# One decode step of attention and MLP: the last 256 KB of wo by six transfers in place of one

## The chip, the cores and the metric

The kernel runs on one core of a Trainium2 chip. The metric is the device time of one execution in microseconds (us); the kernel before takes 102.07 us, the median of 3 runs that lie between 102.06 and 102.33 us. A core has five engines that run their own instruction streams: TensorE (PE, the matmuls; PEld in the profile is its weight load), VectorE (DVE), ScalarE (ACT), GpSimd (POOL) and SyncE (SP, which here only issues transfers). Data comes from HBM into SBUF, which has 128 partitions, by 16 DMA engines that the profile counts together. Matmuls write to PSUM. Engines and transfers wait for one another by semaphores.

## The reference, cut to what matters

```
xn  = layernorm(x)                                # x: [1, 1, 1024]
q   = xn @ wq                                     # 32 heads of 128
k,v = the last 4096 positions of the caches       # 4 kv heads, 8 q heads each
p   = softmax(q k^T / sqrt(128))
o   = p v
A   = o @ wo                                      # wo: [4096, 1024]
y   = layernorm(xn)
h   = gelu(y @ w1 + b1)                           # w1: [1024, 3584]
B   = h @ w2 + b2                                 # w2: [3584, 1024]
out = x + A + B
```

All inputs are bf16. One token is decoded, so every weight and every cache row is used once.

## The kernel before, in words

All large inputs are loaded by SP, one transfer after the other on one queue, in this order: wq in 4 transfers, w1 in 4, the four K blocks, the four V blocks, then w2 in 4 and wo in 7. The first sixteen go out at once. w2 overwrites the buffer of w1 and wo the buffer WA that held wq, so SP waits at L285 until TensorE has finished with w1, and then issues the last eleven (L286, L287) through the helper `load_rows` (L133 to L140; its `dma_start` is L138 in the profile). The issue of the output (L458) comes behind them on the same queue.

`load_rows` gives each partition a run of rows that is contiguous in HBM. wo is seen as [128, 32, 1024]: partition p holds rows 32p to 32p+31, and transfer j brings `WO_CHUNKS[j]` of these 32 to all partitions. `WO_CHUNKS` is [8, 8, 8, 4, 2, 1, 1], so the last transfer brings one row of 1024 bf16 (2,048 bytes) to each of 128 partitions, 256 KB in all. Every transfer has its own semaphore, which stands at 16 when all of it has landed.

TensorE computes q and h as row products (L254), transposes K, takes the scores and, after the softmax, p times v. The output row is held as four pieces of 256 numbers in four groups of 32 PSUM partitions. `out_rows_mms` (L403 to L411, its matmul is L408) adds the products of one chunk of w2 or wo to it: it waits for the semaphore of the chunk and then does 4 matmuls for each row. The chunks of w2 come first (L420, L440, L449), those of wo last, in order (L451, L452). After the last matmul ScalarE copies the row out of PSUM (L456) and SP stores it (L458) and waits until it has landed (L459). The tail of the kernel is therefore: a chunk of wo lands, its matmuls run, and this seven times.

Of the kernel before, what the change touches and what calls it, by code (L numbers as in the profile page):

```python
# [9 lines left out]
D = 1024  # L10
# [12 lines left out]
W1_CHUNKS = [2, 2, 2, 2]  # L23
W2_CHUNKS = [9, 9, 8, 2]
WO_CHUNKS = [8, 8, 8, 4, 2, 1, 1]
PAD = 32


# [12 lines left out]
def bass_parallel_sum__sliding_block_cached__mixer_channel_mlp__decode_kernel(  # L41
# [18 lines left out]
    pe, dve, act, pool, sp = nc.tensor, nc.vector, nc.scalar, nc.gpsimd, nc.sync  # L60

    def sems(name, n):
        return [nc.alloc_semaphore(f"{name}{i}") for i in range(n)]
# [4 lines left out]
    s_k = sems("s_k", HKV)  # L68
    s_v = sems("s_v", HKV)
    s_wo = sems("s_wo", len(WO_CHUNKS))  # L70
    s_w2 = sems("s_w2", len(W2_CHUNKS))

    PE = Track(nc, "S_PE")
# [4 lines left out]
    def sb(name, shape, d):  # L78
        return nc.alloc_sbuf_tensor(name, shape, d)
# [23 lines left out]
    U2 = sb("U2", [128, FC], f32)  # L103
    GT = sb("GT", [128, FC + PAD], bf16)
    MXP = sb("MXP", [128, 32], f32)
    MX32 = sb("MX32", [32, 1], f32)
    DIAG = sb("DIAG", [32, 32], f32)
    NMB = sb("NMB", [128, 32], f32)
    Pb = sb("Pb", [128, HKV * NBLK * REP + PAD], bf16)
    SUMP = sb("SUMP", [128, 128], f32)  # L110
    REC = sb("REC", [128, 1], f32)
    ON = sb("ON", [128, DH], bf16)
    OT = sb("OT", [128, 32 + PAD], bf16)
    KV = sb("KV", [128, HKV * W + HKV * NBLK * DH], bf16)
# [3 lines left out]
    W2 = W1[:, 0:FC * D]  # L118
    WA = sb("WA", [128, KC * NQ], bf16)
# [10 lines left out]
    wo_p = A_wo.rearrange("(p j) n -> p j n", j=32)  # L130
# [4 lines left out]
    def load_rows(dst, src, chunks, width, semaphores):  # L135
        c0 = 0
        for j, n in enumerate(chunks):
            sp.dma_start(  # L138
                dst[:, c0 * width:(c0 + n) * width].rearrange("p (c n) -> p c n", c=n),
                src[:, c0:c0 + n, :],  # L140
            ).then_inc(semaphores[j], 16)
            c0 += n
# [31 lines left out]
    pool.wait_ge(POOL.sem, POOL.cnt)  # L174
    POOL.mark(pool.memset(GT[:, FC:FC + PAD], 0.0))
    pool.wait_ge(POOL.sem, POOL.cnt)
    POOL.mark(pool.memset(OT[:, 32:32 + PAD], 0.0))
    pool.wait_ge(POOL.sem, POOL.cnt)
# [92 lines left out]
    for h in range(HQ):  # L271
        last = pe.matmul(PSb[:, 7 * 1024 + 2 * h: 7 * 1024 + 2 * h + 1], lhsT=Qrow[0:1, h * 128:(h + 1) * 128],  # L272
                         rhs=identb[0:1, 0:1], is_transpose=True)
# [10 lines left out]

    sp.wait_ge(PE.sem, C["h"])  # L285
    load_rows(W2, w2_p, W2_CHUNKS, D, s_w2)  # L286
    load_rows(WA, wo_p, WO_CHUNKS, D, s_wo)  # L287


    KPAIRS = [[0, 1], [2, 3], [4, 5]]  # L290
# [36 lines left out]
    for u in range(NUNIT):  # L327
# [13 lines left out]
        for bb in range(16):  # L341
            o = banks[bb // 8] * 1024 + (bb % 8) * 128
            last = pe.matmul(PSb[:, o:o + 128], lhsT=KT[:, col + bb * 128: col + (bb + 1) * 128],  # L343
                             rhs=identb[:, :], is_transpose=True)
# [16 lines left out]
    for g in range(HKV):  # L361
        if g == HKV - 1:
            wait_kt(pe, 7)
        for b in range(NBLK):
            last = pe.matmul(  # L365
                PS[:, g * 256 + b * 8: g * 256 + (b + 1) * 8],
                lhsT=KT[:, g * W + b * 128: g * W + (b + 1) * 128], rhs=QT[:, g * 8:(g + 1) * 8])
# [32 lines left out]
    def acc(a):  # L400
        return PS[32 * a:32 * a + 32, 6 * 512:6 * 512 + 256]

    def out_rows_mms(weights, vec, chunks, semaphores, j, stop_at=None):  # L403
        c0 = sum(chunks[:j])
        pe.wait_ge(semaphores[j], 16)
        for c in range(c0, c0 + chunks[j]):
            for a in range(4):
                ins = pe.matmul(acc(a), lhsT=vec[:, c:c + 32],  # L408
                                rhs=weights[:, c * D + a * 256: c * D + (a + 1) * 256],
                                start=False, stop=(c == stop_at))  # L410
        return ins  # L411
# [4 lines left out]
    for a in range(4):  # L416
        pe.matmul(acc(a), lhsT=identb[0:1, 0:32], rhs=XBR[0:1, a * 256:(a + 1) * 256], start=True, stop=False)
        pe.matmul(acc(a), lhsT=identb[0:1, 0:32], rhs=XBR[0:1, D + a * 256:D + (a + 1) * 256], start=False, stop=False)
    pe.wait_ge(DVE.sem, C["d_GT"])
    out_rows_mms(W2, GT, W2_CHUNKS, s_w2, 0)  # L420
    pe.wait_ge(DVE.sem, C["sump"])
    C["tot"] = PE.mark(pe.matmul(PS[:, 3 * 512:3 * 512 + 1], lhsT=SUMP[:, :], rhs=onesf[:, 0:1]))
    dve.wait_ge(PE.sem, C["tot"])
# [4 lines left out]
    for g in range(HKV):  # L428
        pe.wait_ge(s_v[g], 16)
        for b in range(NBLK):  # L430
            i = g * NBLK + b
            last = pe.matmul(PS[32 * g:32 * g + 32, 4 * 512:4 * 512 + DH],  # L432
                             lhsT=Pb[:, i * REP:i * REP + 32], rhs=V[:, i * DH:(i + 1) * DH],
                             start=(b == 0), stop=(b == NBLK - 1))
# [2 lines left out]
    dve.wait_ge(DVE.sem, C["rec"])  # L437
    C["on"] = DVE.mark(dve.tensor_scalar(out=ON[:, :], in0=PS[:, 4 * 512:4 * 512 + DH], scalar1=REC[:, 0:1],
                                         scalar2=None, op0=ALU.mult))
    out_rows_mms(W2, GT, W2_CHUNKS, s_w2, 1)  # L440
    pe.wait_ge(DVE.sem, C["on"])
    for dq in range(4):
        last = pe.matmul(PS[:, 5 * 512:5 * 512 + 32], lhsT=E4[:, dq * 128:(dq + 1) * 128],
                         rhs=ON[:, dq * 32:(dq + 1) * 32], start=(dq == 0), stop=(dq == 3))
# [1 line left out]
    dve.wait_ge(PE.sem, C["o2"])  # L446
    C["OT"] = DVE.mark(dve.tensor_copy(OT[:, 0:32], PS[:, 5 * 512:5 * 512 + 32]))
    for j in range(2, len(W2_CHUNKS)):
        out_rows_mms(W2, GT, W2_CHUNKS, s_w2, j)  # L449
    pe.wait_ge(DVE.sem, C["OT"])  # L450
    for j in range(len(WO_CHUNKS)):  # L451
        last = out_rows_mms(WA, OT, WO_CHUNKS, s_wo, j, stop_at=31)  # L452
    C["fin"] = PE.mark(last)

    act.wait_ge(PE.sem, C["fin"])
# [34 lines left out]
```

## Time and profile before

| what | from | value |
|---|---|---|
| median of the runs | times | 102.07 us |
| span of the profiled execution (first to last instruction) | page | 100.8 us |
| time outside the span, median minus span | worked out | 1.27 us |
| bytes read from HBM | page | 39.86 MB, 395 GB/s over the span |
| TensorE busy | page | 69.3 us (69%) |
| idle time of TensorE before L408 with wo, waiting for transfers | groups of instructions | 9.9 us, 6 waits |
| last transfer of wo: SP starts its issue, it lands | timeline of SP, chain | 67.91 us, 98.24 us |
| first and last issue of the output store, end of the span | timeline of SP | 99.15 us, 100.8 us |

The profiled execution's own time is its span with what lies around it; the page gives the span alone, and the 1.27 us are taken as fixed. The page's second part cuts the span into 40 slices; its row DMA is the mean busy share of the 16 DMA engines, in tenths. In the groups of instructions the idle time before a group is put down to what ended it. Beside these views the trace has a record of every packet that a DMA engine moved (start, duration, bytes, queue, but not which of the 16 engines moved it) and of every increment of a transfer's semaphore.

### The profile page before, as it was taken

Reading aid. Unit: us, or ns where it says so; the run is one execution under the profiler, and the core shown is the slowest. Engines: PE = TensorE matmul, PEld = TensorE weight load, DVE = VectorE, ACT = ScalarE, POOL = GpSimd, SP = SyncE. Lnnn points to the kernel's source line nnn. Section 1 sums busy time; section 2 is a strip of 40 time slices with the busy share of each in tenths; the row PEclk is TensorE's granted clock in tenths of the full one; section 3 lists DMA queues with packets and bytes.
Section 4 is the critical chain, followed back from the end, with each engine's and each line's share of the span. In section 5 each row is a group of like instructions: output and inputs, shape, how many; then the busy total and the mean of one; then the engine's idle time right before and its main releaser. Section 6 shows DMA issues by size and latency. Waiting matters only on the chain.

```text
span 100.8 us, 1803 instructions
## 1 busy us (share of the span) xinstructions
PE 69.3 (69%) x825; PEld 42.7 (42%) x825; DVE 21.4 (21%) x46; ACT 13.8 (14%) x16; POOL 4.8 (5%) x18
## 2 busy tenths in 40 slices
PE   0002399999946999996799984649999934070781
PEld 0001233333304223331799984236999823040420
DVE  0003520000054000002876934555000200000000
ACT  0400060000051000002554740040000000000001
POOL 6740000000000000000000000000000000000000
PEclk9999999999996559999999997555559999555555
DMA  4899999999999999999999999999999999999930
GB/s 104 358 442 432 417 436 416 416 431 427 449 432 392 450 427 404 416 416 426 419 423 423 416 431 456 431 395 443 425 398 447 429 423 435 416 422 403 388 139 1
DMA packets 4194, 39.96 MB, mean 396 GB/s; under 512 B 726, under 2 KB 730, under 8 KB 1244
## 3 DMA queue, kind: packets, MB, share of 16 engines
q1 hardware_dynamic: 3896, 39.85, 94.2%
q8 instruction: 6, 0.10, 0.4%
q10 hardware_dynamic: 292, 0.01, 0.2%
HBM read 39.86 MB, written 0.00 MB: 395 GB/s over the span
## 4 chain that ended last, share of the span: by engine, by line
DMA 38%; PE 34%; SPq 20%; DVE 5%; issue 1%; ACT 1%
PE PS L254 31%; DMA WA<-in_A_wo_dram 30%; SPq L138 20%; DMA XB<-in_A_x_dram 7%; DVE ROW L264 2%; PE PS L272 1%; PE PS L234 1%; PE PS L217 1%; PE PS L408 0%; ACT ORow L456 0%; DVE XNT L225 0%; ACT msx L221 0%; DVE msx L198 0%; DVE msy L198 0%; DVE YT L230 0%
## 5 line engine op out<-in xcount | busy, mean ns | idle before, releaser
L254 PE MATMUL PS<-WA,XNTb 128*1 128x512 bf16 x64 | 16.4, 424 | 0.3 <-DVE msy L198 0.3
L254 PE MATMUL PS<-W,YTb 128*1 128x512 bf16 x56 | 15.0, 438 | 0.0
L408 PE MATMUL PS<-WA,OT 128*32 128x256 bf16 x128 | 7.3, 379 | 9.9 <-DMA WA<-in_A_wo_dram 9.9
L254 PEld LDWEIGHTS PS<-WA,XNTb 128*1 128x1 bf16 x64 | 5.8, 91 | 10.5 <-issue 3.5
L408 PEld LDWEIGHTS PS<-WA,OT 128*32 128x32 bf16 x128 | 3.8, 123 | 13.4 <-DMA WA<-in_A_wo_dram 10.3
L432 PE MATMUL PS<-KV,Pb 128*32 128x128 bf16 x128 | 9.2, 260 | 0.0
L254 PEld LDWEIGHTS PS<-W,YTb 128*1 128x1 bf16 x56 | 5.2, 94 | 9.4 <-issue 4.1
L432 PEld LDWEIGHTS PS<-KV,Pb 128*32 128x32 bf16 x128 | 9.1, 119 | 0.0
L343 PE MATMUL PS<-identb,KV 128*128 128x128 bf16 x128 | 7.5, 219 | 1.5 <-ACT ROW L280 1.5
L343 PEld LDWEIGHTS PS<-identb,KV 128*128 128x128 bf16 x128 | 7.1, 98 | 2.0 <-ACT ROW L280 2.0
L217 PE MATMUL PS<-XT,onesf 128*128 128x16 f32 x2 | 0.6, 384 | 8.7 <-DVE XT L213 8.7
L350 DVE COPY KV<-PS 128x1024 bf16<-128x1024 bf16 x10 | 6.3, 684 | 0.7 <-PE PS L343 0.7
L355 ACT ACTIVATE KV<-PS 128x1024 bf16<-128x1024 bf16 x6 | 5.8, 1018 | 1.9 <-PE PS L343 1.9
L408 PE MATMUL PS<-W,GT 128*32 128x256 bf16 x112 | 4.8, 320 | 1.7 <-DMA W<-in_B_w_dram 1.7
L264 DVE CAST ROW<-PS 1x2048 bf16<-1x2048 f32 x1 | 2.3, 2278 | 15.1 <-PE PS L254 15.1
L282 DVE CAST ROW<-PS 1x2048 bf16<-1x2048 f32 x1 | 2.3, 2279 | 14.8 <-PE PS L254 14.8
L456 ACT ACTIVATE ORow<-PS 128x256 bf16<-128x256 f32 x1 | 0.4, 383 | 31.5 <-PE PS L408 31.5
L408 PEld LDWEIGHTS PS<-W,GT 128*32 128x32 bf16 x112 | 3.5, 111 | 2.5 <-DVE PS L386 2.2
L217 PEld LDWEIGHTS PS<-XT,onesf 128*128 128x128 f32 x2 | 0.5, 310 | 8.7 <-DVE XT L213 8.7
L266 ACT ACTIVATE ROW<-PS 1x2048 bf16<-1x2048 f32 x1 | 1.9, 1866 | 14.1 <-PE PS L254 14.1
L280 ACT ACTIVATE ROW<-PS 1x1536 bf16<-1x1536 f32 x1 | 1.4, 1439 | 16.5 <-PE PS L254 16.5
L365 PE MATMUL PS<-QT,KV 128*128 128x8 bf16 x128 | 3.4, 166 | 0.4 <-DVE KV L350 0.4
(75 smaller groups left out, 34.5 us busy)
## 6 DMA issues: line engine op xcount, KB each, us to landing
WA<-in_A_wq_dram SPq DMA_DIRECT2D x4, 2048.0 KB, 14.1
W<-in_B_w_dram SPq DMA_DIRECT2D x4, 1792.0 KB, 30.6
WA<-in_A_wo_dram SPq DMA_DIRECT2D x3, 2048.0 KB, 38.9
W<-in_B_w_dram SPq DMA_DIRECT2D x2, 2304.0 KB, 22.3
KV<-in_A_k_cache_dram SPq DMA_DIRECT2D x4, 1024.0 KB, 39.4
KV<-in_A_v_cache_dram SPq DMA_DIRECT2D x4, 1024.0 KB, 34.4
W<-in_B_w_dram SPq DMA_DIRECT2D x1, 2048.0 KB, 29.3
WA<-in_A_wo_dram SPq DMA_DIRECT2D x1, 1024.0 KB, 42.2
```

The lines of the kernel that those rows point to most:

```text
L138: sp.dma_start(dst[:, c0 * width:(c0 + n) * width].rearrange("p (c n) -> p c n", c=n), src[:, c0:c0 + n, :],).then_inc(semaphores[j], 16)
L217: C["sum1"] = PE.mark(pe.matmul(PS[:, 7 * 512: 7 * 512 + 16], lhsT=onesf[:, :], rhs=XT16[:, 0:16]))
L254: last = pe.matmul(PS[0:1, t * 512:(t + 1) * 512], lhsT=vec[:, k:k + 1], rhs=weights[:, k * width + t * 512: k * width + (t + 1) * 512], s ...
L264: C["d_qrow"] = DVE.mark(dve.tensor_copy(Qrow[:, 0:2048], PS[0:1, 0:2048]))
L266: C["a_qrow"] = ACT.mark(act.activation(out=Qrow[:, 2048:4096], in_=PS[0:1, 2048:4096], func=ACTF.Copy))
L282: C["d_hrow"] = DVE.mark(dve.tensor_copy(Hrow[:, 1536:F], PS[0:1, 1536:F]))
L343: last = pe.matmul(PSb[:, o:o + 128], lhsT=KT[:, col + bb * 128: col + (bb + 1) * 128], rhs=identb[:, :], is_transpose=True)
L350: C["dkt"][u] = DVE.mark(dve.tensor_copy(KT[:, col + 1024 * s: col + 1024 * (s + 1)], PSb[:, bk * 1024:(bk + 1) * 1024]))
L355: C["akt"][u] = ACT.mark(act.activation(out=KT[:, col + 1024: col + 2048], in_=PSb[:, bk * 1024:(bk + 1) * 1024], func=ACTF.Copy))
L365: last = pe.matmul(PS[:, g * 256 + b * 8: g * 256 + (b + 1) * 8], lhsT=KT[:, g * W + b * 128: g * W + (b + 1) * 128], rhs=QT[:, g * 8:(g + ...
L408: ins = pe.matmul(acc(a), lhsT=vec[:, c:c + 32], rhs=weights[:, c * D + a * 256: c * D + (a + 1) * 256], start=False, stop=(c == stop_at))
L432: last = pe.matmul(PS[32 * g:32 * g + 32, 4 * 512:4 * 512 + DH], lhsT=Pb[:, i * REP:i * REP + 32], rhs=V[:, i * DH:(i + 1) * DH], start=(b ...
```

## The change

Transfers 0 to 5 of wo stay as they are. The last row of each partition (column block 31 of WA) is loaded by six transfers, over 75, 28, 12, 8, 4 and 1 partitions, 128 in all, each with a semaphore of its own. Bytes, sources and destinations are the same. TensorE waits for all six semaphores before the last 4 matmuls.

```diff
+TAIL_ROWS = [75, 28, 12, 8, 4, 1]
...
+    s_tail = sems("s_tail", len(TAIL_ROWS))
...
-    load_rows(WA, wo_p, WO_CHUNKS, D, s_wo)
+    load_rows(WA, wo_p, WO_CHUNKS[:-1], D, s_wo)
+    p0 = 0
+    for j, n in enumerate(TAIL_ROWS):
+        sp.dma_start(WA[p0:p0 + n, 31 * D:32 * D], wo_p[p0:p0 + n, 31, :]).then_inc(s_tail[j], 16)
+        p0 += n
...
+    w2_done = [[s] for s in s_w2]
+    wo_done = [[s] for s in s_wo[:-1]] + [s_tail]
+
     def out_rows_mms(weights, vec, chunks, semaphores, j, stop_at=None):
         c0 = sum(chunks[:j])
-        pe.wait_ge(semaphores[j], 16)
+        for sem in semaphores[j]:
+            pe.wait_ge(sem, 16)
...
-    out_rows_mms(W2, GT, W2_CHUNKS, s_w2, 0)
+    out_rows_mms(W2, GT, W2_CHUNKS, w2_done, 0)
...
-        last = out_rows_mms(WA, OT, WO_CHUNKS, s_wo, j, stop_at=31)
+        last = out_rows_mms(WA, OT, WO_CHUNKS, wo_done, j, stop_at=31)
```

More of the change, by code (lines that the diff above doesn't have):

```diff
@@ L439, in bass_parallel_sum__sliding_block_cached__mixer_channel_mlp__decode_kernel @@
                                          scalar2=None, op0=ALU.mult))
-    out_rows_mms(W2, GT, W2_CHUNKS, s_w2, 1)
+    out_rows_mms(W2, GT, W2_CHUNKS, w2_done, 1)
     pe.wait_ge(DVE.sem, C["on"])
@@ L448, in bass_parallel_sum__sliding_block_cached__mixer_channel_mlp__decode_kernel @@
     for j in range(2, len(W2_CHUNKS)):
-        out_rows_mms(W2, GT, W2_CHUNKS, s_w2, j)
+        out_rows_mms(W2, GT, W2_CHUNKS, w2_done, j)
     pe.wait_ge(DVE.sem, C["OT"])
     for j in range(len(WO_CHUNKS)):
-        last = out_rows_mms(WA, OT, WO_CHUNKS, s_wo, j, stop_at=31)
+        last = out_rows_mms(WA, OT, WO_CHUNKS, wo_done, j, stop_at=31)
     C["fin"] = PE.mark(last)
```

## The prediction

> **What bounds the kernel now.** I read the share of the DMA engines over the span first. The page's second part has it, with the bytes per second below it:
>
> ```profile
> DMA  4899999999999999999999999999999999999930
> GB/s 104 358 442 432 417 436 416 416 431 427 449 432 392 450 427 404 416 416 426 419 423 423 416 431 456 431 395 443 425 398 447 429 423 435 416 422 403 388 139 1
> ```
>
> The transfers fill the span at about 420 GB/s, up to the slice before the last two. So the kernel is bound by its loads, and the change is about the end of them. The chain that ended last, in order of time, says what follows the last load:
>
> ```profile
> 56.13 11.73 SPq L138
> 67.87 0.04 issue
> 67.91 30.32 DMA WA<-in_A_wo_dram
> 98.24 0.04 issue
> 98.28 0.43 PE PS L408 x3
> 98.71 0.02 issue
> 98.74 0.38 ACT ORow L456
> ```
>
> The last transfer lands at 98.24, and from there 0.04 + 0.43 + 0.02 + 0.38 us of fixed work and the store follow. What moves 98.24 moves the end, one for one. The timeline of TensorE shows how far 98.24 can move to the left:
>
> ```profile
> 95.74 1.04 PE L408 MATMUL PS<-WA,OT 128*32 128x256 bf16 x16 [0.59 <-DMA WA<-in_A_wo_dram]
> 97.00 1.06 PE L408 MATMUL PS<-WA,OT 128*32 128x256 bf16 x12 [0.22 <-DMA WA<-in_A_wo_dram]
> 98.28 0.41 PE L408 MATMUL PS<-WA,OT 128*32 128x256 bf16 x4 [0.23 <-DMA WA<-in_A_wo_dram]
> ```
>
> TensorE sat idle for only 0.23 us before its last 4 matmuls. The chunk before them (transfer 5, untouched) landed at 97.60 by the records of its semaphore, and its matmuls end at about 98.06. Had the last 256 KB been there at once, the end would come 0.23 us earlier and no more: 101.84. That caps any gain at 0.23%.
>
> Third, the busy time in stretches of half a microsecond (the last two columns are the DMA share and GB/s):
>
> ```profile
> 95.00:95.50 0.50, 0.14 (x4) 0.00 (x0) 0.00 (x0) 0.00 (x0) 0.00 (x0) 0.50 1.00 385
> 95.50:96.00 0.50, 0.26 (x8) 0.21 (x12) 0.00 (x0) 0.00 (x0) 0.00 (x0) 0.50 1.08 414
> 96.00:96.50 0.50, 0.50 (x16) 0.24 (x8) 0.00 (x0) 0.00 (x0) 0.00 (x0) 0.50 0.46 172
> 96.50:97.00 0.50, 0.28 (x9) 0.00 (x2) 0.00 (x0) 0.00 (x0) 0.00 (x0) 0.50 0.41 156
> 97.00:97.50 0.50, 0.50 (x8) 0.13 (x8) 0.00 (x0) 0.00 (x0) 0.00 (x0) 0.50 0.38 147
> 97.50:97.90 0.40, 0.37 (x8) 0.11 (x4) 0.00 (x0) 0.00 (x0) 0.00 (x0) 0.50 0.12 41
> ```
>
> From 96.2 to 97.5 some 0.4 of 16, that is six engines, are at work, and ten have finished. The records of the last semaphore agree: ten increments come between 96.43 and 96.83, six between 97.91 and 98.24. The six are late by about 1.4 us because each has moved one instruction block: the page counts 6 packets on the queue "instruction", at 35.0, 54.3, 62.5, 73.2, 80.6 and 87.5 us by the packet records, 1.02 to 1.10 us each; the last-comers per transfer grow from one after 35.0 to six after 87.5. The records don't say which of the 16 the six are.
>
> **The change, part by part.** *Rows per engine.* A transfer over 128 partitions gave 16 increments; in its tail every engine moved 8 packets of 2,048 bytes, 80 to 83 ns apart, and one completion write, 6 ns. The store over 4 partitions gave 4 packets and 4 increments of landing data, the one-row loads into XBR one packet. I read this as equal shares on as many engines as divide the row count, the same first engines each time: 75 as 5 on 15 engines, 28 as 2 on 14, 12, 8, 4 and 1 as 1 each. No row shows 75 or 28, nor that the engines are the same first ones; a split with a remainder would also put at most 5 and 2 on one engine. The sixteen would then move 11, 10, 10, 10, 9, 9, 9, 9, 8, 8, 8, 8, 7, 7, 5 and 0 rows where all had 8. For a late engine this is worth between +3 x 0.081 + 5 x 0.006 = +0.27 us and, by the cap above, -0.23 us. For a gain the six would have to be those with few rows, and only four have under 8; even set in the best order the six late ends (the fifth's increments, at 1.51, 1.65, 1.69, 1.70, 1.81 and 1.84 us behind its first) give 1.65 + 0.67 = 2.32 behind in place of 1.84 + 0.66 = 2.50, a gain of 0.18. Six drawn from sixteen almost always include one with 9 or 10 rows. I take 9 rows and three more completion writes: +0.10.
>
> *Issues on SP.* Five more `dma_start` on SP's queue. Unblocked ones take 0.43 us (48.94 to 49.37), so 2.2 us at about 72, with only the wait for the output behind them, which comes at 99.15: hidden. Two are blocked in the trace: transfer 5 for 11.73 us and transfer 6 for 4.39 us (67.91 to 72.31), freed about when w2's loads of 66.83 and 72.34 had landed. If each of the five waits for one more landing, they are free at 77.2, 78.5, 83.4, 88.3 and 93.2 (landings by the semaphore records). An issue needs about 1.03 us to its first packet (the first: 0.74 to 1.77), so the sixth starts by 94.2; the first engine ends transfer 5 at 95.36. Cost nothing, with 1.1 us of cover; its loss is rival C.
>
> *Waits on TensorE.* Six semaphores in place of one. Behind the w2 wait of L405 (landing 66.83) the weight load comes at 66.94; two more waits in the trace stand 0.11 us apart (30.69, 30.80 at L269, L270). Waits met earlier cost nothing; those listed behind the last one to be met cost 0 to 0.15. Nothing is queued behind them but the last 4 matmuls, for which ScalarE and SP wait. I take +0.05.
>
> *Rows that cross.* Before, every load was shared out alike, 8 packets an engine, so I take it that each engine always wrote the same 8 partitions. Now ten engines, done with transfer 5 at 95.4, write 75 low partitions while six engines are still 1.4 us behind in theirs, and these six then write rows of other engines. The trace never shows two engines on one another's partitions, so the cost is bounded: nothing (a row stays at 0.08 us), or every one of 8 rows takes twice as long, +8 x 0.084 = +0.67. The nearest row is that of two streams which do meet: the data packet behind each instruction block took 0.46 to 0.53 us longer than its kind (846 against 314 ns, 1,180 against 691). One such meeting for the latest engine, the smallest of them, +0.46, is what I take.
>
> [...] No run here shows a load of part of the partitions.
>
> **The sum.** 0.10 + 0 + 0.05 + 0.46 = +0.61 us on the profiled execution, 98.24 becoming 98.85 and the span 101.4; the median is 1.27 above its span, so 102.07 + 0.61 = 102.68 us.
>
> **The rivals.** *B, no collision.* The rows take 0.08 us wherever they go. For: packets of 2 KB to 18 KB all run at 24 to 27 GB/s, as if the engine alone set it. Against: 26.7 GB/s for 16 engines alike may as well be the limit of the place written to. Time 102.07 + 0.15 = 102.22, with 102.07 to 102.36 as the latest engine has 8 or 10 to 11 rows. This is no change that can be measured (0.3%, about 0.3 us, is what a measurement here tells from none; the three runs differ by 0.27).
>
> *C, the queue.* The last piece is issued too late. It decides from 96.29 on: 98.24 - 0.43 (issue) - 1.03 - 0.09 (row) - 0.43 (last packet to increment: 97.81 to 98.24). If it waits for transfer 4, landed at 96.95, the end is 0.66 later: 102.73. For: the 11.73 us block. Against: the pieces are small, so they should need less room.
>
> *D, the gain.* The late engines are those with few rows, and the tail is there when TensorE is ready: 102.07 - 0.18 to - 0.23 = 101.85. For: six engines are free to be relieved. Against: only four have less to do, and more than 0.23 us would need transfer 5 to land earlier, which the change doesn't touch; it could happen where other executions have fewer late engines.
>
> *E, nothing reaches the end*, as would be if the six pieces were shared out like the one: 102.1, inside B.
>
> **How the numbers follow.** Collision 0.57, B with E 0.27, C 0.06, D 0.10. Slower by over 0.3%: nearly all of the collision case (it needs 0.16 of the 0.46) and C, 0.60. Faster by over 0.3%: half of D, since the cap could be off where the profile isn't the common run, 0.05. The rest, 0.35, is within. The forecast is the collision's 102.68. Its own range is 102.4 to 103.15: with the row count at +0.27, the waits at 0.15 and all rows doubled it is 102.07 + 1.09. The range over all reaches down to the cap, 101.85, and up to 103.1, leaving out the far end of the collision and of D.
>
> **What would show it.** Right: the six semaphores' last increment at about 98.8; late engines' row packets over 0.1 us, or transfer 5's last landing after 97.6; the idle time before the last 4 matmuls 0.23 plus about 0.6. B: packets of 80 to 92 ns and the last increment within 0.2 of 98.24. C: SP's last issue past 96. A late set other than six, or other than the row counts above, shows in the ends per engine. Wrong: if packets to shared partitions aren't slower, the largest term falls; if engines are chosen otherwise, the row counts do.

## The result, and the profile after

The changed kernel takes 103.16 us (median of 4 runs, 103.1 to 103.22) against 102.08 for the kernel before. The ratio is 1.0087 with a 95% interval of 1.007 to 1.0103: slower by 0.7 to 1.0%. The change moves no byte less and no byte more.

The chain that ended last in the changed kernel, in order of time (start, length, what):

```profile
72.25 1.28 SPq L292
73.53 0.04 issue
73.57 1.18 SPq L292
74.75 0.04 issue
74.79 24.21 DMA WA<-in_A_wo_dram
99.00 0.35 issue
99.35 0.32 PE PS L418 x4
99.67 0.02 issue
99.69 0.38 ACT ORow L466
```

Two lines differ from before. The last landing is at 99.00 in place of 98.24, +0.76. Behind it stand 0.35 us of "issue" in place of 0.04, in which TensorE waited for nothing that the chain shows. The four matmuls took 0.32 in place of 0.43, because TensorE had its full clock by then (granted clock 1.00 from 96.73 on, 0.50 before). Together that is 0.76 + 0.31 - 0.11 = 0.96 us, and the span went from 100.8 to 101.8. The rows in which TensorE waits show where the landing became late:

```profile
95.77 1.05 PE L418 MATMUL PS<-WA,OT 128*32 128x256 bf16 x16 [0.59 <-DMA WA<-in_A_wo_dram]
97.64 0.40 PE L418 MATMUL PS<-WA,OT 128*32 128x256 bf16 x8 [0.82 <-DMA WA<-in_A_wo_dram]
98.25 0.29 PE L418 MATMUL PS<-WA,OT 128*32 128x256 bf16 x4 [0.21 <-DMA WA<-in_A_wo_dram]
99.35 0.29 PE L418 MATMUL PS<-WA,OT 128*32 128x256 bf16 x4 [0.81 <-DMA WA<-in_A_wo_dram]
```

The chunk of 16 matmuls (transfer 3) starts at 95.77, as before (95.74). The next one (transfer 4) starts at 97.64 in place of 97.00. Transfer 4 is not part of the change: it is the one that six late engines still carry (increments from 97.11 to 97.59) while the other ten, done with it by 95.39, go on towards the six pieces. The busy time in stretches (DMA share and GB/s last) shows the same moment:

```profile
95.00:95.50 0.50, 0.17 (x4) 0.00 (x0) 0.00 (x0) 0.00 (x0) 0.00 (x0) 0.50 1.02 393
95.50:96.00 0.50, 0.23 (x8) 0.18 (x12) 0.00 (x0) 0.00 (x0) 0.00 (x0) 0.50 0.99 311
96.00:96.50 0.50, 0.50 (x16) 0.28 (x8) 0.00 (x0) 0.00 (x0) 0.00 (x0) 0.50 0.82 201
96.50:97.00 0.50, 0.31 (x8) 0.00 (x0) 0.00 (x0) 0.00 (x0) 0.00 (x0) 0.77 0.40 82
97.00:97.50 0.50, 0.00 (x0) 0.00 (x0) 0.00 (x0) 0.00 (x0) 0.00 (x0) 1.00 0.37 139
```

From 95.5 to 96.0 the 16 engines are about as busy as before (0.99, before 1.08) and move 311 GB/s where they moved 414. From 96.5 to 97.0 six engines are at work in both kernels (0.40 and 0.41), and they move 82 GB/s where they moved 156. The engines spend as much time on their packets and move less by them: the packets take longer. What holds them up is the question of the experiments.

Two kinds of records, read from the trace itself, measure that in every run. The first is the time from the last increment of transfer 3 to that of transfer 4, called landing 3 and landing 4; it leaves out by how much the late engines were late before the tail. The second is the number of packets of 4,096 bytes (transfer 4) that took over 200 ns after 94 us; undisturbed ones take 159 to 171.

| run | ratio to before (95% interval) | landing 3 to landing 4, us | 4 KB packets over 200 ns, longest |
|---|---|---|---|
| before | 1 | 1.26 | 0, 171 ns |
| the changed kernel | 1.0087 (1.007 to 1.0103) | 1.87 | 18, 340 ns |
| the same again (after_again) | 1.0109 (1.0085 to 1.0132) | 1.82 | 17, 326 ns |
| e1_one_sem | 1.0075 (1.0054 to 1.0096) | 1.37 | 20, 282 ns |
| e2_halves | 1.0077 (1.0055 to 1.0099) | 1.96 | 24, 500 ns |
| e3_evenodd | 1.0004 (0.9988 to 1.002) | 1.25 | 0, 171 ns |
| e4_cols | 1.001 (0.9998 to 1.0021) | 1.28 | 0, 171 ns |
| e5_src_halves | 1.0001 (0.9987 to 1.0015) | 1.25 | 0, 171 ns |
| e6_dst_halves | 1.0083 (1.0055 to 1.011) | 1.82 | 20, 408 ns |
| e7_waits | 1.0033 (1.002 to 1.0046) | 1.24 | 0, 171 ns |
| e8_cols_split | 1.0 (0.999 to 1.001) | 1.27 | 0, 171 ns |
| e9_fewer_pe | one run, 102.17 us | 1.25 | 0, 171 ns |
| e10_low64 | 0.9992 (0.998 to 1.0005) | 1.33 | 16, 227 ns |
| e11_mid64 | 0.9952 (0.9935 to 0.9969) | 1.23 | 0, 171 ns |

### The profile page after: what moved, and what is told of

The parts are those of the page before. It is cut to its first block, busy times and chain, and to the rows that moved or that the text cites. A ratio compares the mean times of both kernels' runs of the same rounds, so it can differ in the third digit from the quotient of the medians.

```text
span 101.8 us, 1811 instructions
## 1 busy us (share of the span) xinstructions
PE 66.6 (65%) x825; PEld 41.5 (41%) x825; DVE 21.8 (21%) x46; ACT 13.8 (14%) x16; POOL 4.8 (5%) x18
## 4 chain that ended last, share of the span: by engine, by line
DMA 60%; SPq 33%; PE 3%; issue 1%; ACT 0%
DMA W<-in_B_w_dram 36%; SPq L140 26%; DMA WA<-in_A_wo_dram 24%; SPq L292 7%; PE PS L256 3%; ACT ORow L466 0%; PE PS L418 0%
## 5 line engine op out<-in xcount | busy, mean ns | idle before, releaser
L256 PE MATMUL PS<-W,YTb 128*1 128x512 bf16 x56 | 12.6, 379 | 2.1 <-DMA W<-in_B_w_dram 2.1
L418 PEld LDWEIGHTS PS<-WA,OT 128*32 128x32 bf16 x128 | 4.3, 132 | 15.4 <-DMA WA<-in_A_wo_dram 10.7
L256 PEld LDWEIGHTS PS<-W,YTb 128*1 128x1 bf16 x56 | 4.5, 84 | 9.8 <-DMA W<-in_B_w_dram 3.2
L442 PE MATMUL PS<-KV,Pb 128*32 128x128 bf16 x128 | 8.3, 246 | 0.0
L442 PEld LDWEIGHTS PS<-KV,Pb 128*32 128x32 bf16 x128 | 8.2, 111 | 0.0
L371 PEld LDWEIGHTS PS<-QT,KV 128*128 128x128 bf16 x128 | 3.3, 96 | 0.6 <-DVE KV L356 0.6
```

Of the source, the lines that this page charges most:

```text
L256: last = pe.matmul(PS[0:1, t * 512:(t + 1) * 512], lhsT=vec[:, k:k + 1], rhs=weights[:, k * width + t * 512: k * width + (t + 1) * 512], s ...
L371: last = pe.matmul(PS[:, g * 256 + b * 8: g * 256 + (b + 1) * 8], lhsT=KT[:, g * W + b * 128: g * W + (b + 1) * 128], rhs=QT[:, g * 8:(g + ...
L418: ins = pe.matmul(acc(a), lhsT=vec[:, c:c + 32], rhs=weights[:, c * D + a * 256: c * D + (a + 1) * 256], start=False, stop=(c == stop_at))
```

## The experiments

**The waits.** In the changed kernel all six pieces were counted on one semaphore, so that TensorE has one wait:

```diff
-        sp.dma_start(WA[p0:p0 + n, 31 * D:32 * D], wo_p[p0:p0 + n, 31, :]).then_inc(s_tail[j], 16)
+        sp.dma_start(WA[p0:p0 + n, 31 * D:32 * D], wo_p[p0:p0 + n, 31, :]).then_inc(s_tail, 16)
...
-        for sem in semaphores[j]:
-            pe.wait_ge(sem, 16)
+        for sem in semaphores[j]:
+            pe.wait_ge(sem, 96 if sem is s_tail else 16)
```

> The six pieces as in the changed kernel, but all counted on one semaphore (wait for 96), so that TensorE has one wait in place of six. Against the kernel before at 102.08 and the changed one at 103.16. Theory P (rows that cross into partitions which other engines are still writing slow those engines; the six waits are a smaller part): TensorE starts 0.04 after the last landing in place of 0.32, so 103.16 - 0.28 = 102.9, and the last landing stays at about 99.0. Theory W (the waits are nearly all of it): 102.1 to 102.3. Theory N (six transfers cost something each, whatever they write): 102.9, the same as P.

> The changed kernel once more, beside the experiments of this group, to have its time on the same chip as theirs: 1.07 to 1.10 us over the kernel before. It is also the partner of the run with one semaphore, which stood 0.79 over: 0.3 more than that.

One semaphore: 102.95 us beside 102.16 for the kernel before, +0.79. Six semaphores, run again: 103.24 beside 102.21, +1.03 by the medians and +1.11 by the ratio. So the waits are worth 0.24 us by the medians and 0.35 by the ratios, and are the smaller part. (In the one profile of e1 a single engine stood 2.5 us behind already at the landing of the first wo transfer, at 81 to 84 us, and set the end, so that its landings can't be laid beside the others; the statement rests on the times. From landing 3 to landing 4 this engine took 1.37 us, the other five late increments 1.77 to 1.85.) The other way round, the kernel before got five more waits, all met over 40 us earlier:

```diff
-        pe.wait_ge(semaphores[j], 16)
+        if stop_at is not None and j == len(chunks) - 1:
+            for sem in (s_k[0], s_k[1], s_k[2], semaphores[j], s_k[3], s_v[0]):
+                pe.wait_ge(sem, 16)
+        else:
+            pe.wait_ge(semaphores[j], 16)
```

> The kernel before with one transfer for the last 256 KB, but five more waits of TensorE ahead of its last 4 matmuls, all on semaphores of K and V blocks that were full 40 us earlier; the one that matters stands fourth in the list, as the one that came last did in the changed kernel. If waits that are already met cost time only when they stand behind the last one to be met, and the instructions are laid out as in the changed kernel: the first matmul starts 0.3 us after the landing in place of 0.04, +0.28 us, 102.35. If met waits cost nothing: 102.1.

102.55 beside 102.21, ratio 1.0033 (1.002 to 1.0046). The chain of e7_waits:

```profile
68.16 30.28 DMA WA<-in_A_wo_dram
98.44 0.35 issue
98.79 0.43 PE PS L412 x3
```

The 0.35 us of the changed kernel are there with a single transfer. TensorE's instructions say why. Six waits become three instructions of their own (of one, two and two semaphores) and one that the first weight load carries. The wait fourth in the list, here the only one not yet met, stands first; the other two follow it at 0.11 and 0.22 us, and the weight load at 0.29 us. In the changed kernel that first place falls to the piece of 8 rows, which landed last: its instruction is at 99.03, the weight load at 99.32. So waits that are already met cost 0.29 us here where they stand behind the one that isn't, about 0.1 us for each instruction. Ahead of it a met wait cost nothing in the one place that shows it: in the kernel before, a wait for a K block ahead of a transpose was over at 43.87, and the weight load behind it, held until 48.60, started at 48.64, the same 0.04 us as with a single wait. No run put the last of the six at the end.

**Where rows may be written.** Three ways to load the last 256 KB by two transfers on one semaphore, for whose 32 TensorE waits once. Read as equal shares, 16 increments to a transfer, all leave 8 rows (or 16 half rows) to each engine:

```diff
 # e2_halves
+    for p0 in (0, 64):
+        sp.dma_start(WA[p0:p0 + 64, 31 * D:32 * D], wo_p[p0:p0 + 64, 31, :]).then_inc(s_tail, 16)
 # e3_evenodd
+    for p0 in (0, 1):
+        sp.dma_start(WA[p0:128:2, 31 * D:32 * D], wo_p[p0:128:2, 31, :]).then_inc(s_tail, 16)
 # e4_cols
+    for c in (0, 512):
+        sp.dma_start(WA[:, 31 * D + c:31 * D + c + 512], wo_p[:, 31, c:c + 512]).then_inc(s_tail, 16)
```

> Two transfers, partitions 0 to 63 and 64 to 127, one semaphore: every engine has 8 rows as before (4 and 4), but not its own 8 partitions. P: 102.35 to 102.7, the 4 KB packets of the late engines take more than 0.2 us, transfer 5 lands 0.2 to 0.6 later. Row counts alone (R): 102.1. N: one transfer more than before, a fifth of what five more cost, 102.1 to 102.25.

> Two transfers, even partitions and odd partitions, one semaphore; 8 rows for every engine, and each of the two is spread over all of 0 to 127. If what hurts is that engines write one another's places at all: 102.35 to 102.8, as the halves or more. If it is only that the low 64 partitions are written at once by all engines: 102.1. R: 102.1. N: as the halves.

> Two transfers over all 128 partitions, columns 0 to 511 and 512 to 1023, one semaphore: every engine keeps its own 8 partitions, with packets of 1,024 bytes. P: 102.1 (up to 102.25 if small packets cost more per byte), no packet of 4 KB over 0.18 us. N: the same as the halves.

The halves cost 0.8 us with a single extra transfer and no imbalance. Columns and even/odd rows, two transfers as well, cost nothing that can be measured. So transfer count (N) and row counts (R) fall as main causes. The expectation for even/odd had left both outcomes open; it came out on the side of "only the low 64 at once", though it can't by itself exclude that each engine simply kept its own 8 partitions there.

Halves and even/odd differ on both ends of the transfer, in the rows of HBM that are read and in the partitions that are written. The next two cross them: e5 reads halves and writes even and odd partitions, e6 reads even and odd rows and writes halves.

```diff
 # e5_src_halves
+    for i in (0, 1):
+        sp.dma_start(WA[i:128:2, 31 * D:32 * D], wo_p[64 * i:64 * i + 64, 31, :]).then_inc(s_tail, 16)
 # e6_dst_halves
+    for i in (0, 1):
+        sp.dma_start(WA[64 * i:64 * i + 64, 31 * D:32 * D], wo_p[i:128:2, 31, :]).then_inc(s_tail, 16)
```

> Two transfers whose sources are the HBM rows of partitions 0 to 63 and 64 to 127 and whose destinations are the even and the odd partitions; the last row of wo is thereby applied to other elements of the vector, so the sum is another one, and all other work is the same. If what hurts in the halves is where the data is written (P): as even and odd, the time of before within 0.15 us, no 4 KB packet over 0.18 us. If it is where the data is read: as the halves, +0.8 us.

> The mirror of the last: sources even and odd rows, destinations partitions 0 to 63 and 64 to 127 (the last row of wo meets other elements of the vector here too). P: +0.8 us as the halves, transfer 5 lands 0.5 to 1.0 late, 20 to 24 of the 4 KB packets take over 0.2 us. Reading side: no change.

The cost goes with the written side: 1.0001 and 1.0083. The busy time of e5 in stretches, and then that of e6:

```profile
95.50:96.00 0.50, 0.32 (x8) 0.28 (x12) 0.00 (x0) 0.00 (x0) 0.00 (x0) 0.50 1.03 389
96.50:97.00 0.50, 0.30 (x11) 0.07 (x8) 0.00 (x0) 0.00 (x0) 0.00 (x0) 0.50 0.41 156
```

```profile
95.50:96.00 0.50, 0.14 (x4) 0.00 (x0) 0.00 (x0) 0.00 (x0) 0.00 (x0) 0.50 1.07 316
96.50:97.00 0.50, 0.50 (x12) 0.35 (x13) 0.00 (x0) 0.00 (x0) 0.00 (x0) 0.50 0.38 94
```

With nearly the same DMA share, the engines of e6 move 316 and 94 GB/s where those of e5 move 389 and 156, close to the changed kernel (311 and 82) and to the one before (414 and 156). The changed kernel itself was not crossed in this way; it shares with e2 and e6 the slow packets and the late landing 4.

Last, the same amount to two ranges of 64 partitions; the other half is left out.

```diff
 # e10_low64
+    sp.dma_start(WA[0:64, 31 * D:32 * D], wo_p[0:64, 31, :]).then_inc(s_tail, 16)
 # e11_mid64
+    sp.dma_start(WA[32:96, 31 * D:32 * D], wo_p[32:96, 31, :]).then_inc(s_tail, 16)
```

> Half of the last 256 KB left out: one transfer to partitions 0 to 63 only (4 rows an engine), partitions 64 to 127 keep what lay there. Theory P in its narrow form (a range of partitions is hurt when many engines meet in half of the places, as 0 to 63): slow 4 KB packets (over 0.2 us, 10 to 20) and transfer 5 landing 0.3 to 0.6 late; less bytes take back 0.3 of it, so 102.1 to 102.5. If any range other than one's own hurts alike: the same as the next run.

> The same amount to partitions 32 to 95 (0 to 31 and 96 to 127 left out). [...] If engines hurt one another wherever they leave their own 8 partitions: as 0 to 63.

102.22 against 101.80: with the low 64 the kernel takes 0.42 us more than with the middle 64. TensorE at the end of e10, and of e11:

```profile
96.48 0.64 PE L415 MATMUL PS<-WA,OT 128*32 128x256 bf16 x8
97.41 1.38 PE L415 MATMUL PS<-WA,OT 128*32 128x256 bf16 x16 [0.29 <-DMA WA<-in_A_wo_dram]
```

```profile
96.95 0.40 PE L415 MATMUL PS<-WA,OT 128*32 128x256 bf16 x8 [0.18 <-DMA WA<-in_A_wo_dram]
97.61 0.60 PE L415 MATMUL PS<-WA,OT 128*32 128x256 bf16 x8 [0.26 <-DMA WA<-in_A_wo_dram]
```

Transfer 4 is waited for until 97.41 with the low half and until 96.95 with the middle. Most of this difference is not the tail's: in e10's profile the latest engine was 0.29 us later already when transfer 2 landed (93.48 against 93.19), before any row of the tail moved, and 0.35 at landing 3. From there to landing 4 it took 1.33 us and in e11 1.23; the other five late increments of e10 took 1.37 to 1.54. What is plain is the packets: 16 of transfer 4 were slow with the low half and none with the middle. Another part of the time is the clock (the last matmuls took 0.39 us in e10's profile at a granted clock of 0.50, 0.28 in e11's at 1.00). How much of the 0.42 us is the place of writing isn't shown, nor why the one range slowed packets and the other none.

**The late engines.** The prediction read the six late engines as those that had moved a block of TensorE's instructions. Leaving out 90 matmuls of p times v should keep the sixth block out of the time of the loads:

```diff
-        for b in range(NBLK):
+        for b in (range(NBLK) if g == HKV - 1 else (0, NBLK - 1)):
```

> The kernel before without 90 of the 128 matmuls of p times v (three of four kv heads keep their first and last block only; their part of the sum is left out), so that TensorE has 180 instructions less, under six times 256 in all. If the late engines are late because each has moved one block of TensorE's instructions: five instruction packets in place of six, and five increments of the last transfer 1.3 us or more behind the first in place of six; the time the same as before within 0.3 us, since one late engine is enough. If lateness has another cause: six late as before.

From 30 to 98 us the queue "instruction" moved this in e9, and below it what it moved in the kernel before:

```profile
q8 instruction: 5, 0.08, 0.5%
```

```profile
q8 instruction: 6, 0.10, 0.6%
```

Of the last transfer's 16 increments five come 1.60 to 2.03 us behind the first, the other eleven within 0.71: one block less, one late engine less. No run shows that a block holds 256 instructions, as the expectation reckons: what is recorded is 16,384 bytes for each of the six packets of before. (A sixth block came at 98.5, after the loads.) The time, of a single run, is 102.17, as before: the end goes by the latest engine, not by how many are late.

**A try at a faster kernel.** The column halves with a semaphore each, so that only two matmuls stand behind the last landing:

```diff
+        sp.dma_start(WA[:, 31 * D + c:31 * D + c + 512], wo_p[:, 31, c:c + 512]).then_inc(s_tail[i], 16)
...
             for a in range(4):
+                if tail and a in (0, 2):
+                    pe.wait_ge(s_tail[a // 2], 16)
```

> A try at a faster kernel: the two column halves, each with its own semaphore, the first two matmuls of the last row behind the first half and the last two behind the second. Two matmuls in place of four follow the last landing, about 0.2 us less than the 0.43 of before; smaller packets (46 ns for 1,024 bytes, 85 for 2,048) cost 8 x 7 ns = 0.06 us: 0.1 to 0.15 us faster, 101.95 to 102.0 if before is 102.1. If the second pair starts no earlier because the first pair still runs: no change.

Ratio 1.0 (0.999 to 1.001). The second half landed at 98.36 and its pair ran from 98.40 to 98.80, 0.40 us, as long as the four matmuls of before, 98.28 to 98.69. The four of before write to different groups of PSUM partitions and run side by side (in the records they start within 0.01 us of one another and take 0.39 to 0.40 each); taking two away shortens nothing. No run beats the kernel before with the same work done.

## Why the prediction was right or wrong

The direction held, and the main part of the mechanism as far as the records go: I had rows written by engines that have finished hold up the late ones, and 18 packets of transfer 4, which start between 95.76 and 96.64 us, took 208 to 340 ns where before none took over 171. It was drawn too wide, since I let any row cost that leaves its engine's 8 partitions. No record tells which engine writes which partition, so that crossing itself was not seen, and what the runs show is narrower: slow packets came with writing to halves (e2, e6) or to the low half (e10), and none with even and odd partitions (e3, e5) or with 32 to 95 (e11). The size was short. I had said +0.61 us; the medians differ by 1.08, the interval is 0.71 to 1.05. The median of 103.16 is 0.06 above the upper end of my range; the ratio times 102.07 is 102.96, inside it. In the profile landing 5 is late by 0.61 us, from there to the last landing it takes 0.15 more, the waits take 0.31 (0.28 up to the weight load) and the clock takes 0.11 back: 0.96, where I had added up 0.46 + 0.10 + 0.05 = 0.61.

- *What bounds the kernel*: held. One for one, the last landing moved the end.
- *Rows per engine*: the reading held. The six pieces show 15, 14, 12, 8, 4 and 1 increments of landing data. Late among them are 6, 6, 5, 2, 0 and 0, so by the reading two late engines had 9 rows, three 8 and one 7. The last landing of all, 99.00, is in the piece of 8 partitions, on an engine with 9 rows, as I had taken. From landing 5 to the last it took 0.79 in place of 0.64, +0.15, where I took +0.10; in e2 and e6, where by equal shares every engine has 8 rows, it took 0.59 and 0.62.
- *Issues on SP*: held, and with more cover than I had: all six pieces were issued by 75.7, not 94. Rival C falls. (The terms given for it add up to 96.26, not 96.29, and transfers 1 to 3 were held on the queue too, for 1.84 to 2.14 us; neither matters here.)
- *Waits on TensorE*: the term that was furthest off for its size. I took +0.05 and called 0.15 the end; the first weight load came 0.32 behind the landing in place of 0.04, +0.28. The two rows I used each had one or two wait instructions; the six semaphores here made three (at 99.03, 99.14 and 99.25 us) and a fourth in the weight load (99.32), and the one that stood first was the fourth of the source. The waits of e7 alone cost 0.34.
- *Rows that cross*: right in kind, under-sized. I took one meeting, +0.46, between 0 and 0.67. Landing 5 came 0.61 late (98.21 for 97.60). Per packet it is neither end: those of 4 KB that were slow took 208 to 340 ns in place of 160, most of them about one and a half times as long, and there were 18 of them. The last packet of transfer 4 ended at 96.97 in place of 96.51, +0.46, the very number that I took; but many packets are a little slower, and no single one by that much, so the agreement is luck. Landing 4 followed 0.62 us behind that packet in place of 0.44 (0.50 in the second profile), which no run explains.
- *Not foreseen*: the granted clock. In this profile the last matmuls ran in 0.28 us each in place of 0.40, which took 0.11 back. In the second profile of the changed kernel TensorE waited as long before its last chunks (0.59, 0.77 and 0.78 us; above 0.59, 0.82, 0.21 and 0.81), the granted clock stayed at 0.50 and the span is 101.9. So the waits alone did not bring the clock back, and what did stays open. The end of the second profile:

```profile
97.57 1.04 PE L418 MATMUL PS<-WA,OT 128*32 128x256 bf16 x12 [0.77 <-DMA WA<-in_A_wo_dram]
99.39 0.41 PE L418 MATMUL PS<-WA,OT 128*32 128x256 bf16 x4 [0.78 <-DMA WA<-in_A_wo_dram]
```

- *Rivals B and D* fall with e2 and e6, and with the row counts of the late engines; E falls with those counts too. The cap on a gain was never reached.

## What to carry to other kernels

Splitting a load by ranges of partitions was not free here though it moved the same bytes: halves cost 0.8 us, and columns or even and odd partitions nothing that can be measured (ratios 1.001 and 1.0004). A range across the middle slowed no packet, though it was tried with half of the bytes only. Look at the transfers next to the one that is split, since here the cost fell on one that the change did not touch (landing 3 to landing 4 took 1.87 us in place of 1.26). Where several semaphores gate one instruction on the path that sets the end, use one semaphore for all, which here was worth 0.24 us by the medians; an order in which the one met last stands last was not tried. This change could not relieve the late engines: it did not know which they are, two of them got 9 rows by the reading of their increments, and while the others wrote their rows 18 packets of transfer 4 took over 200 ns. Whether a split that knows the late engines and slows no packet gains anything was not tried either.

## What the runs showed that I had not expected

- A wait instruction already met cost about 0.1 us on TensorE where it stood behind the last one to be met (steps of 0.11, 0.11 and 0.08 us in the changed kernel), and these compiled waits did not stand in the order of the source: the fourth of six came first in the changed kernel and in e7.
- Two matmuls of 128 x 256 into two groups of PSUM partitions took 0.40 us at a granted clock of 0.50 (e8), four into four groups 0.41 (the kernel before).
- The two ranges of 64 partitions were not alike: writing 128 KB to 0 to 63 slowed 16 packets of the transfer ahead of it, writing as much to 32 to 95 none. The runs lie 0.42 us apart, a part of which was there before the tail.
- The late engines differ from run to run in how late they are (in e1 one stood 2.5 us behind where the others stood 1.5 to 1.9), with the same six instruction packets. Why that one was so late, and what places a block on an engine, stays open.
